# Decode attention with a gated MLP: last V in two pieces, wider head sums, longer projection steps, other projection pieces

## Chip, cores, metric

The kernel runs on one core of one Trainium2 chip. The metric is device time in microseconds (us), the median of several executions. Each profile lists two things that are used below: the *span*, from the first to the last instruction recorded, and the time of the execution, which is 1.4 to 2.0 us longer than the span. It also lists the *granted clock* of TensorE (PE), as a share of full speed: below, PE is called *warm* at 1.00 and *cold* at 0.50.

## The reference, cut to what matters

```python
q = (x @ wq) per head                       # 32 heads of 128
scores = q . k_cache * 128 ** -0.5          # k_cache: 32 x 16384 x 128, bf16
o = softmax(scores) @ v_cache               # v_cache: same size
a = o.reshape(1, 4096) @ wo                 # wo: 4096 x 512
b = gated MLP of x (small)
out = g * a + (1 - g) * b                   # g: one sigmoid; 512 values
```

K and V are 134 MB each. Everything else is small, so 279.6 MB have to come from HBM once.

## The kernel before

Heads go in 16 pairs. K of a pair (8 MB) and V of a pair (8 MB) are loads into three rotating buffers, all issued by SyncE in one queue; the projection weights `wo` (4 MB) are the last load. VectorE multiplies K by q, TensorE (PE) sums the products against an identity, ScalarE takes exponentials, PE multiplies them with V, and small fp32 matmuls against `pick` gather a pair's result ("head sums"). After the last pair PE transposes the normalised output, does the first 16 projection rows in a hardware loop ("wide") and the other 16 row by row.

```python
TG = 8                                   # groups of a value step: 8 matmuls of 512 columns
WG = 4                                   # rows of a wide step
V_CUTS = (0, 160, 224, 256)              # pieces of the last V (of 256)
WO_CUTS = (0, 16, 24, 28, 31, 32)        # pieces of wo, in rows of 128x512
WIDE = 16
# ...
def values(e, p, pa, va):                # PE, one pair
    # ...
    with e.Fori(0, NT) as t:             # 8 steps
        # 8 matmuls p8[8 columns] x v8[512], after take(e, v_s): a token of a landed V piece
        ins.then_inc(pv_s, 1)
        fill(e, 8)                       # one matmul of zeros, 0.38 us at full clock
        # register updates
    o2 = o_ps[:, bass.ds(value(e, p, NP - 1) * 2, 2)]
    fill(e, 8, 2)
    take(e, drn_s)                       # ScalarE has copied the sums to d_sb
    for r in range(4):
        ins = e.matmul(o2, lhsT=d_sb[:, r * Dh:(r + 1) * Dh],
                       rhs=pick[:, r * 2:(r + 1) * 2], start=False, stop=False, ...)
    ins.then_inc(pe.sem, 1)              # releases the V buffer
# ...
# loads: load n waits for the user of load n - 3; the last K and V are cut
for a, b, done in zip(cuts[:-1], cuts[1:], sems):
    sp.op(lambda e, ...: e.dma_start(out=buf[n % 3][:, a * Dh:b * Dh], in_=src[:, a * Dh:b * Dh]),
          wait=wait if a == 0 else (), inc=(done, 16))
# ... then wo in its pieces, after the last pair's exponentials
# ...
def pe_wide(e):
    # ...
    warm(e, 3)
    with e.Fori(0, WIDE // WG) as t:
        # WG matmuls of one column x 512, on four column strips of PE; take(e, wo_s) first
        fill(e, 1)
# ScalarE copies the four strips to d_sb; PE adds them with fp32 matmuls after row 24
for j, (a, b) in enumerate(zip(WO_CUTS[:-1], WO_CUTS[1:])):
    for k in range(max(a, WIDE), b):
        y_ok = add(o2[:, k:k + 1], wo[:, k * D:(k + 1) * D],   # two matmuls of 256 columns
                   [(ld_o[j], 16)] if k == a else (), k == H - 1)
    if b == 24:
        add(ones_f[:, 0:1], d_sb[:, :], [w_ok])
# VectorE and ScalarE copy halves of the result; SyncE stores it
```

The softmax here doesn't subtract the row's maximum and nothing guards it: scores larger than these inputs give would overflow.

## Time and profile before

| | before |
|---|---|
| time, median of the first 3 runs | 652.59 us (651.76 to 652.7) |
| span of the profiled run | 650.2 us |
| bytes, rate over the span | 279.6 MB, 430 GB/s |
| last load lands / span ends | 648.2 / 650.2 us |

From the page of the kernel before: engine busy times, the busy tenths of the DMA engines in 40 slices, the load queue (packets, MB, share of 16 engines' span).

```profile
PE 424.3 (65%) x2474; PEld 47.0 (7%) x1312; DVE 335.8 (52%) x159; ACT 45.8 (7%) x112; POOL 2.2 (0%) x10
...
DMA  9999999999999999999999999999999999999998
...
q1 hardware_dynamic: 6194, 279.58, 99.6%
```

The transfers are hardly ever idle: the packets of the load queue take 99.6% of the 16 engines' span, at a mean of 430 GB/s.

The chain of waits of the kernel before, its end (start us, us, what):

```profile
619.02 28.88 DMA bufs<-in_A_wo_dram
647.89 0.04 issue
647.94 0.65 PE ps_all L716 x8
648.58 0.02 issue
648.61 0.41 DVE res L731
```

The one long piece is the fourth piece of `wo`. What follows are the last projection matmuls, the copy of the result and its store.

The DMA issues of the kernel before (KB, us from issue to landing); the first three are pieces of the last V and of `wo`:

```profile
bufs<-in_A_v_cache_dram SPq DMA_DIRECT2D x1, 5120.0 KB, 34.5
bufs<-in_A_v_cache_dram SPq DMA_DIRECT2D x1, 1024.0 KB, 41.0
bufs<-in_A_wo_dram SPq DMA_DIRECT2D x1, 2048.0 KB, 25.4
...
bufs<-in_A_k_cache_dram SPq DMA_DIRECT2D x15, 41.1
bufs<-in_A_v_cache_dram SPq DMA_DIRECT2D x15, 31.1
bufs<-in_A_wo_dram SPq DMA_DIRECT2D x1, 128.0 KB, 28.7
```

At the 430 GB/s of this trace a load of 8.39 MB alone would take 19.5 us. It lands 31 (V) or 41 us (K) after its issue, so I estimate from the differences that a V load has about 11.6 us of other transfers ahead of it, a K load about 21.6 us. By this estimate, that is the margin for a late release of a buffer (E9 takes 4.4 us of it). The last issue of `wo`, at 619.5 us by the timeline, lands 28.7 us later, at 648.2.

PE in the tail of the kernel before, from the timeline (start us, busy us, line, operation). L106 on p_t are value matmuls, L106 on o the wide loop, L716 the last rows:

```profile
631.04 1.02 PE L106 MATMUL ps_all<-bufs,p_t 128*8 x8 [2.03 <-PEq L86]
...
638.42 0.66 PE L106 MATMUL ps_all<-bufs,p_t 128*8 x8
...
643.34 0.39 PE L106 MATMUL ps_all<-bufs,o 128*1 x4 [0.28 <-PEq L86]
644.11 0.39 PE L106 MATMUL ps_all<-bufs,o 128*1 x4 [0.16 <-PEq L86]
...
645.65 0.39 PE L106 MATMUL ps_all<-bufs,o 128*1 x4 [0.19 <-PEq L86]
...
647.23 1.31 PE L716 MATMUL ps_all<-bufs,o 128*1 128x256 bf16 x16
```

The weight loads of PE (PEld) for the last four rows, with the wait before them:

```profile
647.94 0.38 PEld L716 LDWEIGHTS ps_all<-bufs,o 128*1 128x1 bf16 x8 [0.40 <-DMA bufs<-in_A_wo_dram]
```

The last value step ends at 639.1, the wide loop runs from 643.3 to 646.0, the last row ends just before 648.6.

### The profile page before, as it was taken

The numbers are of one execution on the slowest core, as the hardware profiler recorded it, in microseconds if no ns is written. First come the engines' busy times: TensorE is split into PE (matmuls) and PEld (weight loads), VectorE is DVE, ScalarE is ACT, GpSimd is POOL, SyncE is SP. The second block draws the span as 40 slices with busy tenths as digits, with TensorE's granted clock in tenths as the row PEclk, the third lists the DMA queues.
The fourth block names the chain that finished last, engine by engine and source line by source line (L and its number), as shares of the span: only waits on it lengthen the run. The fifth ranks groups of instructions, "written<-read, shape, count | busy, mean of one in ns | idle before, by whom it ended". The sixth has DMA issues, their size and how long they took to land. (4 is left out here: it accounts for less than half of the span.)

```text
span 650.2 us, 7753 instructions
## 1 busy us (share of the span) xinstructions
PE 424.3 (65%) x2474; PEld 47.0 (7%) x1312; DVE 335.8 (52%) x159; ACT 45.8 (7%) x112; POOL 2.2 (0%) x10
## 2 busy tenths in 40 slices
PE   0646687847477574857757486584748857478678
PEld 0000000000101000010000101000010100001022
DVE  3457839256380835628165370835628174465600
ACT  2210000100001000010100001000000100001011
POOL 1000000000000000000000000000000000000000
PEclk9959798958889796888969679796977969698979
DMA  9999999999999999999999999999999999999998
GB/s 384 463 419 452 452 395 443 452 443 395 452 452 395 443 452 448 391 452 452 403 435 452 448 391 452 452 431 407 452 452 395 443 452 439 399 435 468 392 428 342
DMA packets 6203, 279.60 MB, mean 430 GB/s; under 512 B 695, under 2 KB 826, under 8 KB 1210
## 3 DMA queue, kind: packets, MB, share of 16 engines
q1 hardware_dynamic: 6194, 279.58, 99.6%
q8 instruction: 1, 0.02, 0.0%
q10 hardware_dynamic: 8, 0.00, 0.0%
HBM read 279.58 MB, written 0.00 MB: 430 GB/s over the span
## 5 line engine op out<-in xcount | busy, mean ns | idle before, releaser
L579 DVE TENSOR_TENSOR bufs<-bufs,qb x64 | 281.4, 4418 | 170.8 <-DVEq L86 170.8
L91 PE MATMUL ps_all<-bufs,ident 128*128 x960 | 258.8, 423 | 0.0
L496 PE MATMUL ps_all<-bufs,ident 128*128 x64 | 28.6, 446 | 154.2 <-PEq L86 153.9
L106 PE MATMUL ps_all<-bufs,p_t 128*8 x1024 | 82.5, 396 | 30.1 <-PEq L86 20.1
L564 DVE TENSOR_REDUCE s_sb<-ps_all 128x64 f32<-128x512 f32 x64 | 44.0, 687 | 93.1 <-DVEq L86 93.1
L91 PE MATMUL ps_all<-zero,ident 128*8 128x512 bf16 (+2 forms) x167 | 59.5, 388 | 0.0
L592 ACT ACTIVATE p_t<-s_sb 64x256 f32 (+1 forms) x32 | 13.3, 415 | 433.1 <-ACTq L86 432.7
L496 PEld LDWEIGHTS ps_all<-bufs,ident 128*128 128x128 bf16 x64 | 6.3, 99 | 365.6 <-issue 365.6
L106 PEld LDWEIGHTS ps_all<-bufs,p_t 128*8 x1024 | 19.4, 83 | 163.1 <-issue 161.6
L531 PE MATMUL ps_all<-pick,d_sb 128*128 128x2 f32 x128 | 17.0, 255 | 16.5 <-PEq L86 16.5
L531 PEld LDWEIGHTS ps_all<-pick,d_sb 128*128 128x128 f32 x128 | 15.7, 193 | 34.7 <-issue 34.7
L601 ACT COPY d_sb<-ps_all 128x512 f32<-128x512 f32 x16 | 9.4, 586 | 105.4 <-ACTq L86 105.4
L606 ACT CAST ps_all<-zero 128x512 f32<-128x512 bf16 x15 | 8.8, 589 | 1.7
L666 DVE RECIPROCAL rl<-ps_all 128x32 f32<-128x32 f32 x1 | 0.4, 357 | 12.2 <-PE ps_all L552 12.2
L381 DVE TENSOR_TENSOR bufs<-ps_all,ident 128x896 f32<-128x896 f32 x2 | 2.1, 1086 | 8.6 <-PE ps_all L91 8.6
L669 DVE TENSOR_TENSOR o_sb<-ps_all,rl 128x32 bf16<-128x32 f32 x1 | 0.2, 191 | 11.5 <-PE ps_all L531 11.5
L592 ACT ACTIVATION_READ_ACCUMULATOR p_t<-s_sb (+1 forms) x32 | 5.9, 185 | 0.0
L321 PE MATMUL ps_all<-xgw,const-float32-1.0 1*128 1x3 f32 x2 | 0.6, 360 | 8.0 <-DVE xgw L317 8.0
L91 PE MATMUL ps_all<-bufs,xb 128*128 x12 | 5.0, 552 | 0.0
L106 PE MATMUL ps_all<-bufs,u 128*1 x14 | 2.6, 372 | 3.1 <-ACT ps_all L427 2.4
L345 PE MATMUL ps_all<-bufs,xb 128*128 x4 | 2.3, 574 | 3.3 <-DMA bufs<-in_B_w_in_dram 3.3
L106 PE MATMUL ps_all<-bufs,xb 128*64 x32 | 3.6, 380 | 0.0
(76 smaller groups left out, 40.2 us busy)
## 6 DMA issues: line engine op xcount, KB each, us to landing
bufs<-in_A_k_cache_dram SPq DMA_DIRECT2D x2, 4096.0 KB, 36.2
bufs<-in_A_v_cache_dram SPq DMA_DIRECT2D x1, 5120.0 KB, 34.5
bufs<-in_A_wq_dram SPq DMA_DIRECT2D x1, 4096.0 KB, 12.3
bufs<-in_A_v_cache_dram SPq DMA_DIRECT2D x1, 2048.0 KB, 39.0
bufs<-in_A_wo_dram SPq DMA_DIRECT2D x1, 2048.0 KB, 25.4
bufs<-in_B_w_in_dram SPq DMA_DIRECT2D x1, 1792.0 KB, 15.5
bufs<-in_A_v_cache_dram SPq DMA_DIRECT2D x1, 1024.0 KB, 41.0
bufs<-in_A_wo_dram SPq DMA_DIRECT2D x1, 1024.0 KB, 27.6
```

Of the source, the lines that this page charges most:

```text
L91: ins = eng.matmul(out, lhsT=lhsT, rhs=rhs, **flags).ins
L106: ins = eng.matmul(bank[0:m, 0:n], lhsT=lhsT, rhs=rhs, **flags).ins
L321: g_ok = pe.op(lambda e: e.matmul(g_ps, lhsT=ones_f[0:1, :], rhs=xgw[:, :], start=True, stop=True), wait=[xgw_ok], mark=True)
L345: if n else matmul_on(nc, e, lambda: e.matmul(args[0], lhsT=args[1], rhs=args[2], **flags), [at, (xa, 0)]))
L381: dve.op(lambda e, h=h, zh=zh: e.tensor_tensor(out=zm[:, 2 * h * ZB:2 * (h + 1) * ZB].rearrange("p (b m k) -> p b m k", b=2, k=FhC), in0=z ...
L496: matmul_on(nc, e, lambda: e.matmul(s3, lhsT=ident[:, :], rhs=k3[:, :, 0:W], start=True, **flags), [(kw, 0)])
L531: ins = e.matmul(o2, lhsT=d_sb[:, r * Dh:(r + 1) * Dh], rhs=pick[:, r * 2:(r + 1) * 2], start=False, stop=False, skip_group_check=True)
L564: return e.tensor_reduce(out=s_sb[:, c * QK:(c + 1) * QK], in_=s_ps[c % 2].rearrange("p (j w) -> p j w", w=W), axis=AX.X, op=ALU.add)
L579: e.tensor_tensor(out=k3, in0=k3, in1=qi, op=ALU.mult).then_inc(mul_s, 1)
L592: e.activation(out=p_t[rows, bass.ds(at, NG * 8)].rearrange("p (t c) -> p t c", c=8)[:, :, 4 * s:4 * s + 4], in_=s_sb[rows, :].rearrange(" ...
L601: return e.copy(out=d_sb[:, :], in_=d_ps)
L606: e.copy(out=d_ps, in_=zero[:, :]).then_inc(drn_s, 1)
```

## The change

Its intent, as far as the text of it shows: fewer pieces and fewer loop steps at the end, more PE activity in the head sums, and less work behind the last two weight pieces.

```diff
-WG = 4
+WG = 8
-V_CUTS = (0, 160, 224, 256)
-WO_CUTS = (0, 16, 24, 28, 31, 32)
+V_CUTS = (0, 192, 256)
+WO_CUTS = (0, 16, 24, 29, 31, 32)
+PW = 64
-    pick = sb("pick", [P, 4 * 2], FP32)
+    pick = sb("pick", [P, 4 * PW], FP32)
...
+    dve.op(lambda e: e.memset(pick[:, :], 0.0), mark=True)
...
-        out=pick[:, :].rearrange("p (r s) -> p s r", r=4),
+        out=pick[:, :].rearrange("p (r x) -> p x r", r=4)[:, 0:2, :],
...
-        o2 = o_ps[:, bass.ds(value(e, p, NP - 1) * 2, 2)]
+        o2 = o_ps[:, bass.ds(value(e, p, NP - 1) * 2, PW)]
...
-                           rhs=pick[:, r * 2:(r + 1) * 2], start=False, stop=False,
+                           rhs=pick[:, r * PW:(r + 1) * PW], start=False, stop=False,
```

The 62 added columns are zeros, so the result is the same.

## The prediction

> **What bounds the kernel now.** The transfers. The page gives the single load queue 99.6% of 16 engines' span, 279.6 MB at 430 GB/s (PE 65%, DVE 52%). [...] The chain of waits is one piece: the projection weights, issued at 617.7 us, land at 647.9; then 0.65 us of projection matmuls, 0.41 us of the result copy, and the store; the span ends at 650.2. So time is bytes/rate plus a tail of 2.3 us, and the bytes do not change.
>
> **What the change does.**
> 1. Pick widened from 2 to 64 columns. A pair's sums are 8 PE passes in 1.05 us (timeline)[...]. The fp32 projection matmuls stream 256 columns in 0.6 us for four, so I estimate 64 columns add at most 0.03-0.05 us a pass, 0.2-0.4 us a pair. They release a V buffer: the next K is issued that much later. But loads take 31 us (V) and 41 us (K) from issue to landing against 19.5 us of pure transfer at 430 GB/s, so over 10 us of backlog hides it. On critical path: 0. It may keep PE warm over the gap at 629-631 us.
> 2. Last V as 192+64. By the DMA issue list the three pieces land at about 630.8, 635.7 and 638.2 us. The last byte lands at the same 638.2; the first 6 MB piece lands at about 633.3 instead of 630.8. PE steps for it run 1.28 us cold (timeline; clock 0.50 from 630 to 636.8) or 0.65 us warm. Eight steps from 633.4: [...] if warm, about 639, no loss.
> 3. Loop steps of 8. Now four steps, 0.76 us apart, 643.3 to 645.9. Two steps of eight should take about 0.9 us each, as the value steps (8 matmuls and a fill) do. Saves about 1.1 us of PE. It starts when the first weight piece lands (643.1); the normalised output was ready at 642.5. So the loop ends at 645 to 646.1, cancelling step 2's delay.
> 4. Pieces 16, 8, 5, 2, 1. The bytes end at the same time. After the landing of the last but one piece PE does rows 3+1 (8 matmuls, 0.65 us); afterwards 2+1 (6 matmuls, about 0.5 us). PE idled 0.40 us before it. Saves 0 to 0.15 us.
> 5. One issue less, one memset at the start: outside the chain.
>
> **Sum.** About 0.1-0.2 us off a 2.3 us tail: 652.6 - 0.2 = 652.4 us, inside the run-to-run spread (651.8 to 652.7). Range 651.2 to 653.4. Chances: faster by over 2% 0.005, within 2% 0.99, slower 0.005.
>
> **What would show it.** The chain is still the projection weights, landing about 2.3 us before the end; mean rate 429-431 GB/s; pair sums longer by 0.1-0.4 us with unchanged load issue spacing; first value step of the last pair near 633.5; two wide steps of about 0.9 us; six matmuls after the final landing.
>
> **What would make it wrong.** If PE stays cold through the last V's steps, the wide loop and the 5-row piece end after the last landing: up to 1.5 us slower. If piece sizes changed the transfer rate, the whole end would move. A buffer release late enough to drain the load queue would cost more.

In step 2, the end of the value steps if PE starts cold is a term of the forecast: I put that end about 1.4 us later than before, and set the 1.1 us of step 3 against it. With all terms the sum came to 652.6 - 0.2 = 652.4 us, in a range of 651.2 to 653.4.

## The result

The changed kernel took 652.29 us in the median of 6 runs (652.0 to 652.79), the kernel before 651.88 us in 6 runs (651.63 to 652.7). The ratio is 1.0004, with a 95% interval of 0.9991 to 1.0016: the same. Ratios here and below are the mean time of one kernel's runs over that of the other's in the same rounds, so they are not quite the ratio of the medians.

From the page of the changed kernel, the lines shown above of before:

```profile
PE 431.0 (66%) x2473; PEld 45.0 (7%) x1312; DVE 336.5 (52%) x160; ACT 45.8 (7%) x112; POOL 2.2 (0%) x10
...
q1 hardware_dynamic: 6050, 279.58, 99.6%
```

The load queue moves the same bytes in the same share of time, with 144 packets fewer.

The chain of waits of the changed kernel, its end:

```profile
620.52 26.90 DMA bufs<-in_A_wo_dram
647.42 0.04 issue
647.47 1.28 PE ps_all L718 x16
648.75 0.02 issue
648.77 0.41 DVE res L733
```

Its DMA issues:

```profile
bufs<-in_A_v_cache_dram SPq DMA_DIRECT2D x1, 6144.0 KB, 35.6
...
bufs<-in_A_wo_dram SPq DMA_DIRECT2D x1, 2048.0 KB, 23.7
...
bufs<-in_A_v_cache_dram SPq DMA_DIRECT2D x15, 30.8
bufs<-in_A_wo_dram SPq DMA_DIRECT2D x1, 128.0 KB, 26.9
```

PE in its tail:

```profile
633.74 1.02 PE L107 MATMUL ps_all<-bufs,p_t 128*8 x8 [4.45 <-PEq L87]
...
639.25 0.60 PE L107 MATMUL ps_all<-bufs,p_t 128*8 x8
...
640.15 0.60 PE L107 MATMUL ps_all<-bufs,p_t 128*8 x8
...
644.72 0.60 PE L107 MATMUL ps_all<-bufs,o 128*1 x8
...
645.51 0.60 PE L107 MATMUL ps_all<-bufs,o 128*1 x8
...
647.47 1.23 PE L718 MATMUL ps_all<-bufs,o 128*1 128x256 bf16 x16
```

Its weight loads for the last eight rows, pieces of 5, 2 and 1:

```profile
647.46 0.42 PEld L718 LDWEIGHTS ps_all<-bufs,o 128*1 128x1 bf16 x10 [0.56 <-DMA bufs<-in_A_wo_dram]
648.15 0.09 PEld L718 LDWEIGHTS ps_all<-bufs,o 128*1 128x1 bf16 x4 [0.27 <-DMA bufs<-in_A_wo_dram]
648.42 0.08 PEld L718 LDWEIGHTS ps_all<-bufs,o 128*1 128x1 bf16 x2 [0.19 <-DMA bufs<-in_A_wo_dram]
```

The chain above names only the third piece (landing 647.42) and then 1.28 us of PE; the weight loads show that PE waited for each of the last two pieces as well. So the chain alone does not say whether PE or a transfer sets the end: it is PE alone in E4 and E12 too, which are no slower than before, and there the last weight loads waited 0.22 us for `wo`.

Read the two tails against each other. The larger first piece starts the last pair's values 2.7 us later (633.74 against 631.04). They end 1.7 us later (640.75 against 639.08), and the wide loop starts 1.4 us later (644.72 against 643.34). But it has two steps instead of four and is through at 646.11 where it was 646.04 before. From there both kernels wait for `wo`. The last piece lands at 621.5 + 26.9 = 648.4 (before 648.2), and the span ends 2.0 us after it in both. So two changes of more than a microsecond cancelled in front of a transfer that neither moves.

### The profile page after: what moved, and what is told of

It reads as the page before. It is cut to its first block, busy times and chain, and to the rows that moved or that the text cites. A ratio compares the mean times of both kernels' runs of the same rounds, so it can differ in the third digit from the quotient of the medians.

```text
span 650.4 us, 7742 instructions
## 1 busy us (share of the span) xinstructions
PE 431.0 (66%) x2473; PEld 45.0 (7%) x1312; DVE 336.5 (52%) x160; ACT 45.8 (7%) x112; POOL 2.2 (0%) x10
## 3 DMA queue, kind: packets, MB, share of 16 engines
q1 hardware_dynamic: 6050, 279.58, 99.6%
## 5 line engine op out<-in xcount | busy, mean ns | idle before, releaser
L92 PE MATMUL ps_all<-bufs,ident 128*128 x960 | 268.0, 437 | 0.0
L498 PE MATMUL ps_all<-bufs,ident 128*128 x64 | 28.6, 448 | 147.1 <-PEq L87 146.8
L107 PE MATMUL ps_all<-bufs,p_t 128*8 x1024 | 79.1, 384 | 31.6 <-PEq L87 20.9
L92 PE MATMUL ps_all<-zero,ident 128*8 128x512 bf16 (+1 forms) x165 | 57.7, 382 | 0.0
L107 PEld LDWEIGHTS ps_all<-bufs,p_t 128*8 x1024 | 18.0, 82 | 164.3 <-issue 163.7
L533 PE MATMUL ps_all<-pick,d_sb 128*128 128x64 f32 x128 | 17.6, 280 | 16.5 <-PEq L87 16.5
## 6 DMA issues: line engine op xcount, KB each, us to landing
bufs<-in_A_wo_dram SPq DMA_DIRECT2D x1, 2048.0 KB, 23.7
```

What stands on the lines that cost most here:

```text
L92: ins = eng.matmul(out, lhsT=lhsT, rhs=rhs, **flags).ins
L107: ins = eng.matmul(bank[0:m, 0:n], lhsT=lhsT, rhs=rhs, **flags).ins
L498: matmul_on(nc, e, lambda: e.matmul(s3, lhsT=ident[:, :], rhs=k3[:, :, 0:W], start=True, **flags), [(kw, 0)])
L533: ins = e.matmul(o2, lhsT=d_sb[:, r * Dh:(r + 1) * Dh], rhs=pick[:, r * PW:(r + 1) * PW], start=False, stop=False, skip_group_check=True)
```

## The experiments

Twelve kernels ran, all with correct results. "Before" is the kernel before, run in the same rounds on the same chip (9 runs for each set of four, medians 651.72, 651.87 and 651.92 us). E1 to E4 each make one part of the change alone.

### E1: the V pieces alone

```diff
-V_CUTS = (0, 160, 224, 256)
+V_CUTS = (0, 192, 256)
```

> The kernel before with the last V in 192 and 64 only, wide steps of 4. My theory (PE work after the last V is late, and only the shorter wide loop hides it): last value step ends near 640.7 us instead of 639.0, the normalised output is ready near 644.2 instead of 642.5, four wide steps of 0.76 us end near 647.5 instead of 645.9, and the 1.0 us of matmuls for rows 16 to 24, 0.6 us of fp32 matmuls and the last 8 rows end about 1.5 us later than before: +1.0 to +1.7 us. Rival (there is slack enough for each part alone): 0 within 0.4 us.

Measured: 652.48 us against 651.72, ratio 1.0016 (1.0002 to 1.0029); mean span 651.28 against 650.33, so 0.95 us. Just under the low end of my range. The chain of waits of this run no longer has a transfer in it, and none of the weight loads for rows 16 to 31 waits for `wo`:

```profile
646.76 0.39 PE ps_all L106 x4
647.15 0.16 PE ps_all L91
647.31 2.12 PE ps_all L716 x35
649.42 0.02 issue
649.45 0.41 DVE res L731
```

The output was ready 1.6 us later than before (644.16 against 642.54) and about 0.9 us of that reached the end of this profile. The first wide steps ran faster than I assumed (0.60 and 0.75 us apart), so the loop ended at 647.1 and not 647.5. The interval of the ratio starts at 0.1 us, so this run alone does not exclude the rival's 0.4 us. E5 and E6 repeat the loss with the same V pieces (1.2 and 1.1 us of mean span) and E7 has a larger one; with them the rival falls, and so does the upper part of my range.

### E2: the wide steps alone

```diff
-WG = 4
+WG = 8
```

> The kernel before with wide steps of 8 only. My theory: two steps of about 0.8 us in place of four of 0.76, so the loop ends 1.0 to 1.4 us earlier, near 644.7, but the last weight pieces land when they did: time 0 within 0.4 us, and more idle time of PE before the last rows. Rival (the loop is on the path that ends last): -1 us.

Measured: 651.64 us against 651.72, ratio 1.0000 (0.9987 to 1.0014). The loop ended at 644.7, 1.3 us earlier, and PE then waited 0.62 us for the weights of row 16. The gain turned into waiting. The rival falls.

### E3: 64 columns alone

The lines of the diff for `PW`, `pick` and `o2`, nothing else.

> The kernel before with head sums of 64 columns only. My theory: a pair's sums 1.10 us in place of 1.05, issue spacing of the loads and the time unchanged within 0.4 us. Rival (the sums keep the clock up before the last V): the granted clock of the window after the sums of pair 14, 630 to 633.4 us, is above 0.9 and the value steps of the last pair take 0.65 to 0.9 us from the first on. Mine: it is 0.5 there, as before.

Measured: 652.2 us against 651.72, ratio 1.0007 (0.9993 to 1.0020); mean span 650.26 against 650.33. A pair's sums took 1.10 us (1.05 before), and V loads landed 30.9 us after their issue as before. The granted clock in the window from 629.95 to 633.36 us was 0.50, so the sums do not carry the clock over the gap. Time minus span was 1.79 to 1.92 us in all five runs, while most runs of before have about 1.4; more of that below.

### E4: the projection pieces alone

```diff
-WO_CUTS = (0, 16, 24, 28, 31, 32)
+WO_CUTS = (0, 16, 24, 29, 31, 32)
```

> The kernel before with projection pieces of 16, 8, 5, 2, 1 only. My theory: time 0 within 0.4 us; the final matmuls end 0.3 to 0.4 us after the last piece's landing, as before. Rival (piece sizes of the last load change the transfer rate): the last landing moves by more than 0.5 us against the end of the last V's transfer.

Measured: 651.96 us against 651.72, ratio 1.0006 (0.9993 to 1.0020). The last piece landed at 648.1 (620.4 + 27.7), the matmuls ended at 648.4 to 648.5, 0.3 to 0.4 us later. The piece came 9.96 us after the landing of the last V (before 9.95), so no change of rate is seen, and no gain from having less work behind the last two pieces.

### E5: the V pieces alone, with PE kept warm

```diff
 V_CUTS = (0, 192, 256)
...
             e.matmul(l_ps[:, 0:H], lhsT=ones_f[:, :], rhs=L_sb[:, :], start=True,
                      stop=True).then_inc(sl_s, 1)
+            warm(e, 18)
```

> The kernel with only the V pieces changed, plus 18 matmuls of 128x512 zeros (about 3.9 us at full clock) while PE waits for the first piece of the last V. Clock theory (as my prediction had it): the value steps then run at 0.65 us from the first on, the last ends by 639.4 instead of 640.6, and the time returns to the kernel before within 0.3 us. Rival [...]: steps 0.90 us apart from near 633.5, the last ends at 640.3 to 640.9, and the time stays that of the V pieces alone, +0.6 to +1.1 us over before.

(The rival: its figures are those of the trace of before: 0.90 to 0.95 us a step in the steady pairs, and 0.65 us only after steps of 1.28.)

Measured: 652.98 us against 651.87, ratio 1.0018 (1.0004 to 1.0031); mean span 651.66 against 650.42, so 1.24 us, a little over the rival's range. Windows of this run (PE busy, weight loads, other engines; the last three columns are granted clock, DMA share, GB/s), then its timeline:

```profile
629.95:633.40 3.45, 3.01 (x14) 0.00 (x0) 0.00 (x0) 0.00 (x0) 0.00 (x0) 1.00 0.87 375
633.40:640.60 7.20, 6.40 (x72) 1.07 (x64) 0.00 (x0) 0.00 (x0) 0.00 (x0) 1.00 1.01 430
```

```profile
633.53 0.60 PE L106 MATMUL ps_all<-bufs,p_t 128*8 x8 [0.57 <-PEq L86]
...
634.44 0.60 PE L106 MATMUL ps_all<-bufs,p_t 128*8 x8
...
635.39 0.60 PE L106 MATMUL ps_all<-bufs,p_t 128*8 x8
...
639.95 0.61 PE L106 MATMUL ps_all<-bufs,p_t 128*8 x8
```

The 18 added matmuls took 4.04 us (628.91 to 632.95). The clock was full from the first step on (1.00 in both windows), and still the steps were 0.90 to 0.95 us apart and the last ended at 640.56, where the cold start of E1 ended at 640.7. The clock theory, which was mine in the prediction, falls. What the traces show is the order of the paces. Where PE started cold (before, at a granted clock of 0.50; E1, with the same 0.63 us for a fill), a step took 1.28 us, and the steps just after that followed 0.65 us apart, with fills of 0.38 us and, in before, a clock of 0.98. Where the clock was full from the first step on (1.00 here, and in the steady pair of before from 510.1 to 517.0 us), they came 0.90 to 0.95 us apart. Over eight steps both come to nearly the same (7.03 us here, 7.28 in E1). The changed kernel has both: after its faster steps the last three start at 638.35, 639.25 and 640.15, at a full clock (1.00 from 636.8 to 640.6), so 0.90 us apart again. Why the first steps after cold ones come sooner, and what sets the 0.90 us, is not shown; no run took instructions out of the step. After the first, the wide steps of this run were 0.95 to 0.97 us apart where those of E1 were 0.75 to 0.79, so its tail is even longer than that of E1. I don't know why. The runs with the old V pieces give a second sign that the clock was worth little: a fill took 0.38 us again at 635.02 in E4 (0.62 to 0.63 cold) and 0.40 only at 636.81 in E2, the output was ready at 642.40 in both, and in E4 PE stood idle for 0.75 us before its last value step, whose piece landed at 638.1.

### E6: the changed kernel with wide steps of 4

```diff
-WG = 8
+WG = 4
```

> The changed kernel with wide steps of 4 again. Theory (the wide steps repay the late V pieces): the wide loop starts near 644.7 and takes about 2.5 us, the chain that ends last is PE alone from there on, and the time is 0.5 to 1.1 us over before. Rival (the loss seen with the V pieces alone was chance): within 0.3 us of before.

Measured: 653.33 us against 651.87, ratio 1.0023 (1.0010 to 1.0037). The span is 651.52 us in the mean, 1.10 us over the 650.42 of before in the same rounds, and 1.05 us over the 650.47 of the changed kernel's own, earlier runs. The loop ran from 644.67 to 647.2, and the chain is PE alone from there. The rest of the 1.46 us between the medians is outside the span. This is E1 again from the other side: without the longer steps the late V pieces show.

### E7: the changed kernel with the last V in one piece

```diff
-V_CUTS = (0, 192, 256)
+V_CUTS = (0, 256)
```

> The changed kernel with the last V in one piece, a larger dose of the same delay. Theory: the piece lands near 638.6, eight value steps from there end near 646, 5.3 us after the changed kernel's, of which little is hidden any more: +4 to +5.5 us over before. Rival (the tail is set by transfers only): within 0.5 us.

Measured: 656.52 us against 651.87, ratio 1.0074 (1.0058 to 1.0089); span +4.5 us in the mean. Its chain:

```profile
650.89 2.01 PE ps_all L718 x33
652.90 0.02 issue
652.92 0.41 DVE res L733
```

The value steps started at 638.30 and the output was ready at 648.83, 4.6 us later than in the changed kernel; 4.1 us of that reached the end of this profile (654.5 against 650.4). So about half a microsecond of a PE delay is hidden in the changed kernel, and about 0.7 us (1.6 less 0.9, E1) in the kernel before. E12 agrees by chance: its output was ready 0.6 us later than before (643.14), and its span was still 650.1 us. The last load still landed at 648.1.

### E8: the wide steps and the projection pieces, without the rest

```diff
-WG = 4
+WG = 8
-WO_CUTS = (0, 16, 24, 28, 31, 32)
+WO_CUTS = (0, 16, 24, 29, 31, 32)
```

> The kernel before with wide steps of 8 and projection pieces of 16, 8, 5, 2, 1, V pieces and head sums as before: the parts that cannot delay PE. Theory: last matmuls end about 0.35 us after the last landing; 0 to -0.3 us against before, not to be told from noise. Rival (shorter PE work in the tail still pays): -1 us.

Measured: 651.83 us against 651.87, ratio 0.9996 (0.9982 to 1.0010). The best that the parts give is not to be told from the kernel before. The span ends 2.0 us after the last landing.

### E9: the changed kernel with late head sums

```diff
     def drain(e, late=False):
         take(e, pv_s, NT)
+        if late:            # inside the loop over pairs only
+            e.copy(out=junk[:, :]..., in_=zero[:, :]...)     # 128x4096
```

> The changed kernel with one extra ScalarE copy of 128x4096 values (estimate 4.4 us, from 0.59 us for 512 columns) before each drain of the pairs inside the loop, so that a pair's sums, and with them the release of a V buffer, come some 4 us later, 80 times the 0.05 us that the wider sums added. Theory (over 10 us of queued transfers hide a late release): K loads are issued some 4 us later after their V loads, 13.5 us instead of 9.3, land in 37 us instead of 41, DMA share stays 99%, time within 0.5 us of the changed kernel. Rival (releases are on the path): about 14 x 4 = 56 us slower.

Measured: 651.67 us against 651.92, ratio 0.9998 (0.9985 to 1.0012). The copy took 3.6 us (my estimate was 4.4), and the sums that followed it took 1.96 us. Issues of SyncE in one pair of this run, then the landing of the K loads:

```profile
470.83 0.33 SPq L644 DMA_DIRECT2D bufs<-in_A_v_cache_dram  x1
484.53 0.33 SPq L644 DMA_DIRECT2D bufs<-in_A_k_cache_dram  x1
```

```profile
bufs<-in_A_k_cache_dram SPq DMA_DIRECT2D x15, 36.1
```

A K load was issued 13.7 us after its V load, not 9.3, and landed 36.1 us after its issue, not 41: what the issue lost the queue gave back. A release that is 4.4 us late costs nothing here, so neither do the 0.05 us of the wider sums.

### E10: head sums of 256 columns

```diff
-PW = 64
+PW = 256
```

(on top of E3)

> The kernel before with head sums of 256 columns. Theory [...]: a pair's sums take 1.2 to 1.9 us; issue spacing and span as before, +0 to +0.4 us of span; mean granted clock at or above 0.86. Open question: time minus span was 1.4 us in 22 of 22 runs of e1, e2, e5, e8 and most runs of before, but 1.8 to 2.0 in most runs of the kernels with 64 columns. If wider streaming makes this, 1.9 here too.

(The 22 runs named there were 20.) Measured: 652.16 us against 651.92, ratio 1.0004 (0.9990 to 1.0018). A pair's sums:

```profile
558.73 1.99 PE L533 MATMUL ps_all<-pick,d_sb 128*128 128x256 f32 x8 [1.07 <-PEq L87]
```

1.99 us, a little over my range: the passes come (1.99 - 0.379) / 7 = 230 ns apart, where the last pass takes 0.379 us; with 64 columns they are 118 ns apart, and only the columns changed. The mean granted clock of its runs is 0.889, against 0.844 for before in the same rounds, and in this profile the clock stayed at 1.00 over the gap before the last V. The first five value steps were then 0.90 to 0.94 us apart, as in E5; two of the last three waited for their pieces. More clock and no less time. The profiled run has a span of 651.5 us: its last load landed at 649.3, 1.1 us later than before, and PE, whose output was ready only at 644.6, no longer waited for it. The other four are at 650.3 to 650.8.

### E11 and E12: where the time outside the span comes from

E11 lays `pick` out and zeroes it 64 columns wide, but streams 2 columns. E12 is the kernel before with one more tile of the same size, zeroed at the start and not used.

> The head-sum tile laid out and zeroed 64 columns wide, but 2 columns streamed. If the 0.45 us outside the span comes from the streaming: time minus span back to 1.4 us. If from the tile or its zeroing: 1.9 us. If it is chance of a run: a mixture. Span as before within 0.4 us, sums 1.05 us.

> The kernel before with one more tile of 128x256 fp32 zeroed by VectorE at the start and used by nothing. If the zeroing at the start makes the 0.45 us outside the span: time minus span 1.9 us. Otherwise 1.4 us, or a mixture if it is chance. Span as before within 0.4 us.

Measured: E11 652.2 us (ratio 1.0005, 0.9991 to 1.0019), E12 652.05 us (1.0002, 0.9988 to 1.0016), spans as before. Time minus span:

| kernels | runs with 1.75 us or more |
|---|---|
| before, all rounds of E1 to E12 | 7 of 27 |
| no extra zeroing: E1, E2, E5, E8 / E4 | 0 of 20 / 3 of 5 |
| extra zeroing: the changed kernel, E3, E6, E7, E10, E11, E12 | 31 of 35 |
| E9 (extra zeroing, further code) | 1 of 5, the others 1.52 to 1.57 |

The streaming is not the cause (E11). Kernels with the extra zeroing at the start mostly show the longer remainder (E12), but E4 has it without and E9 mostly lacks it. The profile shows nothing outside the span, so the cause stays open. The mean of time minus span is 1.82 us in the six runs of the changed kernel and 1.54 us in the 27 of before, which is most of the 0.41 us between the medians of the two kernels.

## Why the prediction was right, and where it was not

- **What bounds it: right.** In every profile but that of E10 (649.3) the last load lands between 648.0 and 648.8 us, whatever PE does. What differs is how long after it the span ends: 2.0 us in before, in the changed kernel, in E2 and E4, 3.0 in E1, 3.3 in E5, 2.8 in E6, 6.5 in E7.
- **Step 1, the sums: right that it is free, wrong in size.** I put 0.2 to 0.4 us a pair; it is 0.05 (1.10 against 1.05). I had added the streaming to each pass. The passes stay 0.11 to 0.12 us apart: (1.05 - 0.251) / 7 = 114 ns with 2 columns and (1.10 - 0.275) / 7 = 118 ns with 64, where the last pass takes 0.251 and 0.275 us. So from 2 to 64 columns the streaming does not set the pace; with 256 the passes are 230 ns apart (E10). What sets it below that is not shown: the record of a single weight load lasts 186 to 192 ns, the loads overlap, eight in 0.97 us, and no run separates the load from other costs of a pass. That the sums may keep PE warm over the gap did not come true: the granted clock over 629.95 to 633.4 us was 0.53 with 2 columns (before) and 0.50 with 64 (E3 and the changed kernel). Only in the profile with 256 columns did it stay up (E10), and there the gap before the first value step was also shorter, 0.5 us instead of 2.0.
- **Step 2, the last V: right in direction.** First step at 633.7 (said 633.4), last end at 640.75, so 1.7 us late; the term from step 2 had 1.4 us for a cold start. The step "if warm, about 639, no loss" was wrong: in E5 the warm steps came 0.90 to 0.95 us apart, not 0.65, and ended at 640.6 with a full clock.
- **Step 3, the wide loop: right.** I said two steps of about 0.9 us and a saving of 1.1 us, with the end between 645 and 646.1; the loop took 1.4 us instead of 2.7 and ended at 646.11. E2 and E6 show both halves: alone it gives nothing, and without it the change loses 1.05 us of span. One detail was wrong: in the changed kernel the loop starts when the output is ready (644.3), not when the first weights land (619.67 + 23.7 = 643.4).
- **Step 4, the projection pieces: the expected 0 to 0.15 us came to nothing.** The last matmul ended 0.4 us after the last landing before and after. I had counted eight matmuls behind "the last but one piece", but the last piece lands some 0.3 us later still, and only its one row is behind it in both kernels.
- **The sum.** Said 652.4, measured 652.29, in a range set by the noise of runs. That close a hit is luck: I took 0.2 us off a median of three runs (652.59) that six runs put at 651.88. The 0.2 us gain against before was not there: spans are within 0.1 us (650.47 in the mean of 6 runs, 650.40 for the 27 runs of before in the later rounds), and about 0.3 us came from outside the span, of which the prediction knew nothing. What was not luck is the balance: a late start and a shorter loop that cancel in front of the weights.

## What to carry to other kernels

When one queue of transfers is busy for 99.6% of the span, look only at what follows the last landing and at whether any release comes later than the backlog of the queue; a change of microseconds elsewhere can leave the time as it is: here a loop end 1.3 us earlier turned into waiting (E2), and a release 4.4 us later cost nothing (E9). Parts of a change that cancel (a PE start 1.7 us later, a loop 1.3 us shorter) look like "no effect" together, and one run of each part alone tells them apart from parts that truly do nothing. For short loop steps, measure the pitch of steps that run at full clock from the first on (0.90 to 0.95 us in E5), not that of the steps just after a cold start (0.65 us in before and E1).
